# A linear-attention scan feeding an FFN: a different written order for the first 42 FFN tasks and the work around them

## The chip, the cores and the metric

One core of a Trainium2 chip runs the whole program. It has TensorE (PE, with its weight loads shown as PEld), VectorE (DVE), ScalarE (ACT), GpSimd (POOL) and SyncE (SP), which here only issues transfers. The metric is the device time of one execution in microseconds (us). "Runs" below are executions that were timed; the profile is of one execution.

## The reference

For every batch and head a 48x48 state is carried over 768 time steps, and the result goes through an FFN with a sigmoid-approximated GELU.

```
for t in range(S):                                   # r,k,v,w: (4, 8, 768, 48), u: (8, 48)
    cur = einsum('bhd,bhe->bhde', u[None] * kt, vt)
    y[:, :, t] = einsum('bhd,bhde->bhe', rt, state + cur)
    state = wt[:, :, :, None] * state + einsum('bhd,bhe->bhde', kt, vt)
x = y.transpose(0, 2, 1, 3).reshape(3072, 384)
h = x @ w_in                                         # (3072, 384) @ (384, 2048)
g = h * (1 / (1 + exp(-1.702 * h)))
out = g @ w_out                                      # (3072, 2048) @ (2048, 384)
```

## The kernel before, in words

The 3072 tokens are 24 chunks of 128. A chunk `t` is one run of the generator `chunk`, which yields between 13 parts. In order they are: a scan on DVE (L330, with the small L333); a second scan (L335); the product kq (L341); four transposes on PE (L348) and their copy kt on ACT (L350); rku (L356, DVE); ps_d (L368, PE); the copy s and eight small am operations on ACT (L371, L378); ps_u (L398, L402, PE); the state (L408 to L412, DVE); a predicated copy into am (L415, DVE); ps_y (L425, L438, PE) and a one-element copy on ACT that follows it (L448); the other half of L438; and the split of the result into a high and a low part x (L271 on ACT, L272 on DVE). Chunks 0 and 1 are kept whole instead (L462), and split later (L471, L473). From chunk 8 on rku and ps_d are replaced by L359 to L361 and L383 on DVE.

The FFN runs as tasks: task `j` is a group of chunks and one of 16 blocks of the hidden width. Its first product on PE is `g` (L502 to L504: high weights by both halves of x, low weights by the high half), its GELU is `h` (L519 and L520 on ACT, and the difference gl on DVE, L522), its second product is `y` (L540 to L542). Tasks 0 to 4 are done in plain float32 (L497, L512, L537) before their weights are split. Tasks 0 to 9 cover two chunks (256 columns), task 10 and later four chunks (512).

Weights arrive in 12 pieces of 1024 KB: `f` issues the transfer of a piece into one of three staging buffers, `w` converts it in four parts (L253 and L254 on ACT; L256 and L259 on DVE; the high part on ACT, L263; the low part on DVE, L267). The last DVE instruction of the second part lets the buffer go. `l` issues the loads of a chunk, `m` is a check sum on ACT (L277), `x` moves 16 rows of finished x between partitions with small transfers from SP and POOL (L481), `s` splits chunks 0 and 1, `d` followed by a number arranges that the next PSUM bank taken is first written by that many products of a constant tile (L305, "warm", 128x512 in bfloat16, results never used). Five PSUM banks go round, first freed, first taken; a bank is free when ACT or DVE has read it.

Engines run their instructions in the order in which the program issues them. That order is written out by hand in the string `RAMP`: each token is one part of the above (`a3` is the next part of chunk 3, `g5` the first product of task 5). After its last token, which belongs to task 41, a rule (`rest`) gives the order of the remaining tasks. Every queue is in order, SP's too: a load that waits for its buffer holds up the loads behind it.

Of the kernel before, what the change touches and what calls it, by code (L numbers as in the profile page):

```python
# [79 lines left out]
BEFORE = 9  # L80
FIRST = 42
RAMP = """
l0 M l1 l0 a0 a0 a0 d26 a0 l0 a1 a0 d6 a0 f0 m0 a0 a0 l2 a1 l1 a1 l2 a0 a1 m1 a1 d6 a1 l3 a1 a0 a2 a1 a0 a1 a0 a1 w0
l3 a2 a1 a0 a2 a3 d5 a2 a1 a1 f1 w1 f2 x1 a2 a3 d4 a2 a3 a2 a2 l4 a3 a2 a3 d5 a3 w0 f3 a3 a3 a2 a3 m2 a3 g0 h0 g1 w2
l4 w1 a2 h1 a3 w2 a4 a2 f4 w3 a2 w2 w3 a3 a3 x3 y0 y1 w2 g2 g3 h2 w1 h3 f5 g4 w0 h4 a4 s0 y2 w4 w0 y3 y4 m3 g5 s0 a4
w4 h5 w3 w1 a4 w3 a4 w5 g6 h6 g7 g8 g9 l5 w5 h7 y5 f6 w4 l6 f7 w4 a4 a4 a4 h8 a5 w5 y6 f8 w5 y7 h9 a5 w6 g10 g11 g12
h10 y8 y9 a5 y10 h11 w6 w7 h12 w6 a4 w6 y11 a4 a5 a5 g13 h13 g14 f9 y12 w7 m4 g15 l5 a5 w8 h14 a4 w8 h15 w7 a5 w7
g16 g17 y13 a6 h16 y14 y15 y16 w9 a6 h17 w9 f10 f11 g18 g19 m5 h18 a5 w8 a4 a5 h19 a5 w8 w10 y17 a6 l7 w9 y18 y19
w11 g20 a7 l7 w9 a6 a6 w10 h20 g21 g22 w11 h21 w10 l6 w11 a6 a6 y20 w10 w11 a4 h22 u y21 g23 a7 h23 a5 a6 a6 a5 l8
a7 m7 a6 m6 a8 g24 a7 a7 a5 a8 y22 a7 h24 a6 a7 a7 a6 a7 l8 a8 y23 l9 a7 a6 a8 l9 a8 m8 a8 a7 l10 a9 a8 l10 a8 a7 a7  # L90
a9 x7 a9 g25 y24 h25 y25 a9 a9 a8 a8 a10 a10 g26 g27 h26 y26 a9 a9 l11 h27 a8 a9 a9 m9 a8 a10 g28 a11 y27 a9 a10 a10
a10 a10 g29 a8 a11 h28 a9 a10 l11 a9 a11 h29 y28 a10 a11 y29 g30 a11 a9 a11 m10 a10 a11 a11 a11 a11 h30 l12 a10 a11
l13 a10 a10 a11 y30 a12 a12 m11 a11 g31 a12 l14 a13 a13 g32 g33 h31 g34 y31 g35 g36 h32 h33 h34 a13 m12 y32 h35 g37
a12 y33 h36 y34 y35 y36 h37 y37 g38 g39 g40 h38 g41 h39 h40 y38 y39 h41
"""
WIDE = 512
GAP = 64
# [703 lines left out]
```

## Time and profile before

| | |
|---|---|
| runs | 502.23, 501.39, 503.08 us; median 502.23 |
| profiled execution | 501.6 us from the first to the last instruction |
| PE busy | 489.3 us, 98% |
| PE weight loads | 405.8 us, 81% |
| DVE / ACT / POOL busy | 294.2 us (59%) / 227.2 us (45%) / 15.4 us (3%) |
| mean granted TensorE clock | 0.995 of 2.4 GHz |
| moved by DMA | 45.82 MB |

Busy time counts overlapping instructions of an engine once. The page gives the span alone for the profiled execution, and it lies inside the range of the runs. Averages over the whole span hide that the first 160 us and the rest are different: the chunks' and the weights' work on DVE and ACT lies mostly in the first part.

### The profile page before, as it was taken

The numbers are of one execution on the slowest core, as the hardware profiler recorded it, in microseconds if no ns is written. First come the engines' busy times: TensorE is split into PE (matmuls) and PEld (weight loads), VectorE is DVE, ScalarE is ACT, GpSimd is POOL, SyncE is SP. The second block draws the span as 40 slices with busy tenths as digits, with TensorE's granted clock in tenths as the row PEclk, the third lists the DMA queues.
The fourth block names the chain that finished last, engine by engine and source line by source line (L and its number), as shares of the span: only waits on it lengthen the run. The fifth ranks groups of instructions, "written<-read, shape, count | busy, mean of one in ns | idle before, by whom it ended". The sixth has DMA issues, their size and how long they took to land.

```text
span 501.6 us, 11866 instructions
## 1 busy us (share of the span) xinstructions
PE 489.3 (98%) x5036; PEld 405.8 (81%) x5036; DVE 294.2 (59%) x502; ACT 227.2 (45%) x526; POOL 15.4 (3%) x48
## 2 busy tenths in 40 slices
PE   8989999999999999999999999999999999999996
PEld 4668999887887888888888888888888878888884
DVE  8889999989898314765655555655655521111211
ACT  2889899775444324432342442342442332322221
POOL 2001000001001000000001000001000001000000
PEclk9989999999999999999999999999999999999999
DMA  7884988056532500261104171104040001100001
GB/s 200 259 214 138 221 263 226 23 151 185 173 83 55 136 0 3 95 190 48 48 3 126 45 208 49 51 1 126 23 138 1 1 1 31 64 0 0 1 0 70
DMA packets 26508, 45.82 MB, mean 91 GB/s; under 512 B 3952, under 2 KB 17712, under 8 KB 26448
## 3 DMA queue, kind: packets, MB, share of 16 engines
q1 hardware_dynamic: 25472, 42.94, 30.5%
q0 software_dynamic: 864, 1.66, 1.4%
q8 instruction: 41, 0.67, 0.6%
q10 hardware_dynamic: 112, 0.39, 0.3%
q14 instruction: 19, 0.16, 0.1%
HBM read 38.00 MB, written 4.72 MB: 85 GB/s over the span
## 4 chain that ended last, share of the span: by engine, by line
PE 87%; DVE 8%; DMA 2%; issue 1%; ACT 1%; SPq 0%; DVEq 0%; ACTq 0%
PE po L540 12%; PE ph L502 12%; PE ph L504 12%; PE ph L503 12%; PE po L542 12%; PE po L541 12%; PE ps_y L438 2%; PE ps_y L425 2%; PE ps_u L402 2%; PE ph L497 2%; PE ps_u L398 2%; DMA wkr_t<-in_wkr 2%; PE ps_t L348 2%; PE po L537 1%; DVE lp L330 1%
## 5 line engine op out<-in xcount | busy, mean ns | idle before, releaser
L522 DVE TENSOR_TENSOR gl<-gf,gh 128x512 fp32r<-128x512 f32 (+1 forms) x101 | 65.7, 650 | 158.2 <-ACT gf L520 157.2
L519 ACT ACTIVATE gh<-ph 128x512 fp32r<-128x512 f32 (+1 forms) x101 | 57.1, 566 | 204.9 <-PE ph L504 193.8
L502 PE MATMUL ph<-x,h 128*128 128x512 f32 (+1 forms) x303 | 115.6, 382 | 0.7 <-DVE am L415 0.7
L504 PE MATMUL ph<-x,l 128*128 128x512 f32 (+1 forms) x303 | 113.4, 374 | 0.0
L540 PE MATMUL po<-gh,h 128*128 128x512 f32 (+1 forms) x297 | 113.3, 381 | 0.0
L503 PE MATMUL ph<-x,h 128*128 128x512 f32 (+1 forms) x303 | 113.2, 373 | 0.0
L542 PE MATMUL po<-gl,h 128*128 128x512 f32 (+1 forms) x297 | 111.2, 374 | 1.2 <-DVE gl L522 1.2
L541 PE MATMUL po<-gh,l 128*128 128x512 f32 (+1 forms) x297 | 110.9, 374 | 0.0
L502 PEld LDWEIGHTS ph<-x,h 128*128 128x128 f32 x303 | 57.0, 188 | 10.8 <-PE po L542 0.9
L542 PEld LDWEIGHTS po<-gl,h 128*128 128x128 f32 x297 | 55.9, 188 | 12.0 <-DVE gl L522 1.9
L504 PEld LDWEIGHTS ph<-x,l 128*128 128x128 f32 x303 | 57.0, 188 | 10.4
L503 PEld LDWEIGHTS ph<-x,h 128*128 128x128 f32 x303 | 57.1, 188 | 9.6
L540 PEld LDWEIGHTS po<-gh,h 128*128 128x128 f32 x297 | 55.9, 188 | 10.4
L541 PEld LDWEIGHTS po<-gh,l 128*128 128x128 f32 x297 | 56.0, 188 | 9.3
L520 ACT ACTIVATE gf<-ph 128x512 f32<-128x512 f32 (+1 forms) x101 | 56.7, 562 | 4.6 <-DVE gl L522 4.6
L330 DVE TENSOR_TENSOR_SCAN lp<-wkr_t,d1r 112x516 f32<-112x516 f32 x24 | 29.4, 1226 | 1.0 <-DMA wkr_t<-in_wkr 1.0
L341 DVE TENSOR_TENSOR kq<-wkr_t,lp 112x1024 f32<-112x1024 f32 x24 | 29.3, 1221 | 0.9 <-PE ps_y L438 0.6
L335 DVE TENSOR_TENSOR_SCAN lp<-wkr_t,d1f 112x516 f32<-112x516 f32 x24 | 29.5, 1229 | 0.5
L350 ACT COPY kt<-ps_t 128x448 f32<-128x448 f32 (+1 forms) x24 | 12.7, 530 | 34.4 <-PE ps_t L348 34.4
L277 ACT ACTIVATE junk<-lp 112x1032 bf16<-112x1032 f32 x24 | 25.5, 1063 | 0.0
L438 PE MATMUL ps_y<-kq,mid 64*64 64x64 f32 (+3 forms) x384 | 22.9, 218 | 0.8 <-ACT mid L448 0.4
L481 POOL DMA_DIRECT2D x<-x x18 | 9.0, 507 | 380.1 <-DVE x L272 269.2
(101 smaller groups left out, 517.5 us busy)
## 6 DMA issues: line engine op xcount, KB each, us to landing
st<-in_w_out SPq DMA_DIRECT2D x6, 1024.0 KB, 6.0
rk_t<-in_vrk SPq DMA_DIRECT2D x16, 384.0 KB, 4.3
st<-in_w_in SPq DMA_DIRECT2D x6, 896.0 KB, 8.6
v_t<-in_vrk SPq DMA_DIRECT2D x24, 192.0 KB, 3.7
out_t<-ob SPq DMA_DIRECT2D x15, 256.0 KB, 2.3
wkr_t<-in_wkr SPq DMA_DIRECT2D x18, 192.0 KB, 3.2
wkr_t<-in_wkr SPq DMA_DIRECT2D x36, 96.0 KB, 3.4
wkr_t<-in_wkr SPq DMA_DIRECT2D x5, 577.9 KB, 4.8
```

The costliest lines, as they stand in the source:

```text
L330: V.tensor_tensor_scan(li[:, ::-1], w1[:, ::-1], d1r.rearrange("r p c -> r (p c)")[:, ::-1], 0.0, op0=ALU.mult, op1=ALU.add)
L335: V.tensor_tensor_scan(pm, w0, d1f.rearrange("r p c -> r (p c)"), 0.0, op0=ALU.mult, op1=ALU.add)
L438: T.matmul(ps[b][head(h), p], from_[head(half), p * D + OFF * h : p * D + HB], qf[head(half), p, blocks[b]], start=False, stop=p == PAIRS[ ...
L502: T.matmul(ph, h_, xs[i][:, 0, c, cs], start=c == 0, stop=False)
L503: T.matmul(ph, h_, xs[i][:, 1, c, cs], start=False, stop=False)
L504: T.matmul(ph, l_, xs[i][:, 0, c, cs], start=False, stop=c == NM - 1)
L519: A.activation(gh, ph, AF.Gelu_apprx_sigmoid, scale=1.0 / W_SCALE)
L520: A.activation(gf, ph, AF.Gelu_apprx_sigmoid, scale=1.0 / W_SCALE)
L522: V.tensor_tensor(gl, gf, gh.bitcast(F32), op=ALU.subtract)
L540: T.matmul(o, h_, gh, start=first, stop=False, skip_group_check=True)
L541: T.matmul(o, l_, gh, start=False, stop=False, skip_group_check=True)
L542: T.matmul(o, h_, gl, start=False, stop=f == NF - 1, skip_group_check=True)
```

## The change

The string `RAMP` is replaced. Both strings issue the same parts of the same chunks, pieces and tasks, and end at the same point, so the program after task 41 is the same. Only the order differs, and the numbers behind `d`: 52 dummy products before (26, 6, 6, 5, 4, 5), 60 after (36, 1, 9, 3, 1, 3, 2, 2, 3). No function changes.

```diff
 RAMP = """
-l0 M l1 l0 a0 a0 a0 d26 a0 l0 a1 a0 d6 a0 f0 m0 a0 a0 l2 a1 l1 a1 l2 a0 a1 m1 a1 d6 a1 l3 a1 a0 a2 a1 a0 a1 a0 a1 w0
-l3 a2 a1 a0 a2 a3 d5 a2 a1 a1 f1 w1 f2 x1 a2 a3 d4 a2 a3 a2 a2 l4 a3 a2 a3 d5 a3 w0 f3 a3 a3 a2 a3 m2 a3 g0 h0 g1 w2
...
+d2 d34 l0 M l0 a0 a0 l0 l1 a0 a0 a0 d1 f0 l2 l1 m0 a0 a0 a0 a1 a1 a1 a0 a0 d9 a1 a1 a1 m1 a1 a1 a0 a0 a2 a1 a2 l3 l2 w0
+a1 d3 a0 a1 a2 a3 a0 a1 a1 f1 a2 a2 a3 w1 l3 f2 x1 d1 a3 a2 a2 a2 a3 l4 a3 w0 a3 d3 f3 a3 l4 m2 a2 a2 a3 a3 a3 g0 h0
...
```

SP issues the transfers. In these rows, from some 12 us to some 26 us, `wkr_t` and `v_t` are a chunk's inputs, `st` a weight piece and the last row of shuffles the `x` of chunks 0 and 1. Before:

```order
L214 DMA v_t_86<-in_vrk 128x384
L198 DMA wkr_t_83<-in_wkr 96x1541
L214 DMA v_t_84<-in_vrk 128x384
L235 DMA st<-in_w_out 128x2x1024
L233 DMA st<-in_w_in 112x2x1024
L233 DMA st<-in_w_in 16x2x1024
L481 DMA l_384<-l_384 16x256 x3
```

After:

```order
L198 DMA wkr_t_83<-in_wkr 96x1541
L214 DMA v_t_86<-in_vrk 128x384
L235 DMA st<-in_w_out 128x2x1024
L214 DMA v_t_84<-in_vrk 128x384
L233 DMA st<-in_w_in 112x2x1024
L233 DMA st<-in_w_in 16x2x1024
L481 DMA l_399<-l_399 16x256 x3
```

The piece of w_out has moved ahead of the load into `v_t_84`, which has to wait until ps_y of chunk 0 has read that buffer. Further down the same queue the piece `f5` has moved ahead of the shuffles of chunks 2 and 3 (`x3`) in the same way.

DVE, around 33 to 43 us, behind the am copies of chunk 3; `h_416` and `h_425` are piece 1, `l_580` and `l_582` piece 2. Before:

```order
L256 SCALAR_TENSOR_TENSOR st<-st 128x1024
L259 SCALAR_TENSOR_TENSOR h_416<-h_416,st 128x1024
L256 SCALAR_TENSOR_TENSOR st<-st 128x1024
L259 SCALAR_TENSOR_TENSOR l_580<-l_580,st 128x1024
L330 SCALAR_TENSOR_TENSOR lp<-wkr_t_82,d1r 112x516
L333 RECIPROCAL d1f<-lp 112x4
L272 TENSOR_TENSOR x<-ps_y_586,x 112x4x64
```

After:

```order
L256 SCALAR_TENSOR_TENSOR st<-st 128x1024
L259 SCALAR_TENSOR_TENSOR h_425<-h_425,st 128x1024
L330 SCALAR_TENSOR_TENSOR lp<-wkr_t_82,d1r 112x516
L333 RECIPROCAL d1f<-lp 112x4
L256 SCALAR_TENSOR_TENSOR st<-st 128x1024
L259 SCALAR_TENSOR_TENSOR l_582<-l_582,st 128x1024
L272 TENSOR_TENSOR x<-ps_y_617,x 112x4x64
```

The first scan of chunk 4 now stands between the two pieces. Just behind, the product kq of chunk 4 (L341) has moved ahead of the low part of piece 0 (L267), and the split of chunks 0 and 1 (L473) behind it.

PE, ahead of ps_y of chunk 4 (some 75 us). Before:

```order
L502 MATMUL ph<-x,h_847 128x256
L503 MATMUL ph<-x,h_847 128x256
L504 MATMUL ph<-x,l_859 128x256
L368 MATMUL ps_d<-hm,rku 128x2 x4
L425 MATMUL ps_y_1131<-am,v_t_85 48x64
```

After:

```order
L540 MATMUL po_650<-gh,h_949 128x256
L541 MATMUL po_650<-gh,l_951 128x256
L542 MATMUL po_650<-gl,h_949 128x256
L305 LDWEIGHTS warm
L305 MATMUL ps_y_1126<-warm 128x512
L305 LDWEIGHTS warm
L305 MATMUL ps_y_1126<-warm 128x512
L425 MATMUL ps_y_1126<-am,v_t_85 48x64
```

Two dummy products stand there now, and the second product of task 12 comes before ps_y instead of after it. In the same way two dummies stand before the transposes of chunk 8 and three before ps_y of chunk 7.

## Rows read from the trace of the kernel before

**Rows 1.** The page: busy time of the engines.
```profile
PE 489.3 (98%) x5036; PEld 405.8 (81%) x5036; DVE 294.2 (59%) x502; ACT 227.2 (45%) x526; POOL 15.4 (3%) x48
```

**Rows 2.** Windows: length, then busy us of PE, PEld, DVE, ACT, POOL, clock, DMA.
```profile
200.00:250.00 50.00, 50.00 (x565) 41.32 (x564) 31.50 (x65) 19.41 (x44) 0.00 (x0) 1.00 0.33 96
```

**Rows 3.** Waits from 0 to 165 us: us in total, times, longest.
```profile
ACT st L253 <- DMA st<-in_w_out: 2.3, 3, 1.0
PE po L542 <- DVE gl L522: 1.2, 2, 0.9
```

**Rows 4.** Timeline of PE at the start: begin, length, instruction, idle before.
```profile
1.14 7.46 PE L305 MATMUL ps_t<-warm 128*128 128x512 bf16 x26 [1.14 <-DVE warm L119]
9.39 0.57 PE L348 MATMUL ps_t<-ident,kq 112*128 112x112 f32 x4 [0.79 <-DVE kq L341]
12.22 0.62 PE L398 MATMUL ps_u<-v_t,kt 64*64 64x48 f32 x30
```

**Rows 5.** Timeline of PE's weight loads, from the first rise of the clock.
```profile
4.53 3.57 PEld L305 LDWEIGHTS <-warm 128*128 128x128 bf16 x17 [0.28 <-issue]
```

**Rows 6.** Timeline of DVE, 14 to 21 us.
```profile
14.84 0.36 DVE L412 TENSOR_TENSOR sf<-ps_u,mid 112x192 f32<-112x192 f32 x1 [1.25 <-ACT mid L406]
20.89 1.23 DVE L341 TENSOR_TENSOR kq<-wkr_t,lp 112x1024 f32<-112x1024 f32 x1
```

**Rows 7.** Timeline of ACT, 10 to 15 us.
```profile
10.43 1.07 ACT L277 ACTIVATE junk<-lp 112x1032 bf16<-112x1032 f32 x1
12.59 2.02 ACT L378 ACTIVATE am<-same,s 128x64 f32<-128x64 f32 x8
```

**Rows 8.** Issues on SP, timeline.
```profile
18.91 0.43 SPq L235 DMA_DIRECT2D st<-in_w_out  x1
24.30 1.88 SPq L481 DMA_DIRECT2D l<-l  x3
```

**Rows 9.** DMA issues up to 165 us: times, size of one, median us to landing.
```profile
x<-x POOLq DMA_DIRECT2D x3, 32.0 KB, 2.0
l<-l POOLq DMA_DIRECT2D x3, 16.0 KB, 6.3
```

**Rows 10.** Windows: the last three columns are clock, share of DMA engines, GB/s.
```profile
16.00:20.00 4.00, 3.64 (x138) 3.47 (x142) 3.76 (x10) 3.32 (x13) 0.00 (x0) 1.00 0.69 177
20.00:31.00 11.00, 9.70 (x222) 7.03 (x216) 10.52 (x15) 9.20 (x31) 1.60 (x3) 1.00 0.99 261
41.00:46.00 5.00, 5.00 (x25) 4.40 (x24) 4.96 (x8) 4.74 (x12) 0.89 (x2) 1.00 0.00 0
```

**Rows 11.** Timeline of PE, 27 to 46 us.
```profile
27.08 1.24 PE L305 MATMUL ps_d<-warm 128*128 128x512 bf16 x5
30.13 0.62 PE L398 MATMUL ps_u<-v_t,kt 64*64 64x48 f32 x30 [0.71 <-ACT s L371]
31.62 4.51 PE L497 MATMUL ph<-l,l 128*128 128x256 f32 x12 [0.33 <-DVE am L415]
41.70 4.05 PE L497 MATMUL ph<-l,l 128*128 128x256 f32 x18
```

**Rows 12.** Windows of one microsecond.
```profile
32.00:33.00 1.00, 1.00 (x4) 0.82 (x3) 0.90 (x4) 1.00 (x2) 0.00 (x0) 0.50 0.45 162
```

**Rows 13.** Timeline of DVE, 36 to 51 us.
```profile
36.89 1.23 DVE L256 SCALAR_TENSOR_TENSOR st<-st 128x1024 int32<-128x1024 int32 x1 [1.27 <-ACT l L254]
48.13 0.95 DVE L473 TENSOR_TENSOR x<-l,x 128x768 fp32r<-128x768 f32 x1
50.13 1.22 DVE L256 SCALAR_TENSOR_TENSOR st<-st 128x1024 int32<-128x1024 int32 x1
```

**Rows 14.** Timeline of PE: task 5 begins, and two waits later on.
```profile
49.28 0.47 PE L502 MATMUL ph<-x,h 128*128 128x256 f32 x1
72.67 0.36 PE L502 MATMUL ph<-x,h 128*128 128x256 f32 x1 [0.68 <-DVE am L415]
82.09 0.39 PE L542 MATMUL po<-gl,h 128*128 128x256 f32 x1 [0.32 <-DVE gl L522]
```

More of the change, by code (lines that the diff above doesn't have):

```diff
@@ L82 @@
 RAMP = """
-l0 M l1 l0 a0 a0 a0 d26 a0 l0 a1 a0 d6 a0 f0 m0 a0 a0 l2 a1 l1 a1 l2 a0 a1 m1 a1 d6 a1 l3 a1 a0 a2 a1 a0 a1 a0 a1 w0
-l3 a2 a1 a0 a2 a3 d5 a2 a1 a1 f1 w1 f2 x1 a2 a3 d4 a2 a3 a2 a2 l4 a3 a2 a3 d5 a3 w0 f3 a3 a3 a2 a3 m2 a3 g0 h0 g1 w2
-l4 w1 a2 h1 a3 w2 a4 a2 f4 w3 a2 w2 w3 a3 a3 x3 y0 y1 w2 g2 g3 h2 w1 h3 f5 g4 w0 h4 a4 s0 y2 w4 w0 y3 y4 m3 g5 s0 a4
-w4 h5 w3 w1 a4 w3 a4 w5 g6 h6 g7 g8 g9 l5 w5 h7 y5 f6 w4 l6 f7 w4 a4 a4 a4 h8 a5 w5 y6 f8 w5 y7 h9 a5 w6 g10 g11 g12
-h10 y8 y9 a5 y10 h11 w6 w7 h12 w6 a4 w6 y11 a4 a5 a5 g13 h13 g14 f9 y12 w7 m4 g15 l5 a5 w8 h14 a4 w8 h15 w7 a5 w7
@@ L88 @@
[L88 to L92, printed above, removed]
@@ L93 @@
-l13 a10 a10 a11 y30 a12 a12 m11 a11 g31 a12 l14 a13 a13 g32 g33 h31 g34 y31 g35 g36 h32 h33 h34 a13 m12 y32 h35 g37
-a12 y33 h36 y34 y35 y36 h37 y37 g38 g39 g40 h38 g41 h39 h40 y38 y39 h41
+d2 d34 l0 M l0 a0 a0 l0 l1 a0 a0 a0 d1 f0 l2 l1 m0 a0 a0 a1 a1 a1 a0 a0 d9 a1 a1 a1 m1 a1 a1 a0 a0 a2 a1 a2 l3 l2 w0
+a1 d3 a0 a1 a2 a3 a0 a1 a1 f1 a2 a2 a3 w1 l3 f2 x1 d1 a3 a2 a2 a2 a3 l4 a3 w0 a3 d3 f3 a3 l4 m2 a2 a2 a3 a3 a3 g0 h0
+g1 w2 w1 a2 a4 a3 h1 w2 y0 a2 a3 f4 g2 w3 a3 w3 f5 w1 w2 a2 w0 g3 x3 y1 a4 g4 h2 h3 h4 l5 w2 y2 w4 s0 y3 a4 f6 w0 w3
@@ new lines @@
+y4 w4 s0 g5 h5 w1 m3 a4 g6 h6 a4 w5 g7 l6 g8 y5 a4 w3 f7 w5 w4 h7 w4 a4 g9 h8 a5 a4 y6 y7 g10 w5 w5 h9 a5 w6 y8 g11 y9
+h10 a5 y10 h11 w6 g12 g13 w7 a4 h12 g14 w6 a5 w6 f8 h13 w8 y11 a4 g15 a5 m4 w7 d2 h14 y12 w8 a4 w7 a5 h15 g16 w7 f9 l5
+a5 a6 y13 y14 h16 f11 w9 a6 g17 h17 y15 a4 g18 w9 y16 f10 m5 g19 h18 a5 l7 w8 a5 a5 y17 h19 y18 w9 w10 w8 y19 a6 w11
+g20 a6 w9 g21 w10 h20 w11 g22 l6 a6 w10 h21 w11 a7 l7 h22 y20 w11 a6 a6 y21 a5 w10 g23 a4 a7 h23 a6 u a5 a7 a6 m6 l8
+m7 a6 a8 g24 a7 a7 a5 a8 y22 a7 h24 a6 a7 a7 a6 a7 l8 y23 a8 d2 a6 a8 l9 a7 l9 a8 m8 d3 a7 l10 a8 a9 a8 a8 a7 a7 g25
@@ L95 @@
+x7 a8 y24 a9 h25 a9 y25 a8 a9 a9 g26 h26 g27 y26 l10 a9 a10 a9 a10 h27 a8 a9 a9 a8 m9 y27 a10 a8 l11 a11 g28 a9 a10
+a11 a10 h28 a10 g29 a9 a10 a10 l11 a9 y28 a11 h29 a10 a11 y29 g30 a11 a9 m10 a10 a11 a11 a11 a11 a11 h30 l12 a10 a11
+a12 y30 a12 l13 a10 a12 l14 a11 a11 m11 g31 a10 g32 h31 a13 g33 g34 g35 m12 a13 g36 y31 h32 h33 a13 h34 y32 h35 a12
+y33 h36 y34 g37 g38 y35 y36 h37 y37 g39 g40 h38 h39 h40 g41 y38 h41 y39
 """
```

## The prediction

> **What bounds the kernel.** The page first: PE is busy for 98% of the span, the others far less [rows 1]. Busy PE is not PE at its best, so I looked at windows: in a stretch well behind the change PE is busy for all of 50 us at the full clock [rows 2]. What the change can move therefore lies in the first 160 us, as dummy products, waits and slow clock on PE. Everything PE needs there less than before ends the kernel earlier by as much, since the later tasks follow each other without a gap.
>
> The list of waits and PE's timeline say where this is. At the start PE runs 26 dummies and then waits for the first kq [rows 4]. Around 30 us it waits for ps_u of chunk 3 and for the first real task [rows 11], and that task runs at half clock: 0.50 granted, 1.2 of 2.4 GHz [rows 12]. Its 12 products took 4.51 us, where later 18 took 4.05 [rows 11], so some 1.8 us are lost. Later there are three waits for DVE: 0.68 us at 72.67, 0.32 at 82.09 [rows 14] and one of 0.9, the longest for gl [rows 3]; its place in the timeline is near 124 us. Between 20 and 100 us DVE hardly rests, and its own largest idle stretch after the start is 1.27 us at 36.89, waiting for ACT [rows 13]. That is the limit which I followed through the new order.
>
> **The start.** The dummies begin at 1.14. From 4.53 on their weights follow each other at 3.57/17 = 0.21 us [rows 5], so ten more hold the first transposes from 9.39 [rows 4] to about 10.6. PE gets most of this back: five dummies fewer follow, and rku now comes right behind the first kq, so that ps_u of chunk 0 starts near its old 12.22 [rows 4]. ACT doesn't: the check sum of 1.07 us starts 1.04 us behind the transposes [rows 4, 7], now at 11.65, ends at 12.75 or so with its small read, and only then come s and the eight am of 2.02 us, so that am starts at about 12.95 in place of 12.59 [rows 7]. DVE, which waits for ACT there, gets going again at 15.2, not 14.84 [rows 6]. Moving the second scan of chunk 2 ahead of an am copy hides a short latency between scan and kq, so I take **+0.2 us** at the kq that stood at 20.89 [rows 6]; the bounds are 0.1 and 0.4.
>
> **Transfers to the first task.** The piece of w_out was issued at 18.91 [rows 8] behind a load that waits for ps_y of chunk 0. Now it stands behind a load without a wait and goes out near 17. From 16 to 20 us the DMA engines were 0.69 busy, from 20 to 31 us 0.99 [rows 10]: 0.31 x 4 = 1.2 us of room, so all that follows lands up to 1.2 us earlier. Two things gain. ACT waited up to 1.0 us for such a piece [rows 3], which put off kt and s of chunk 3, hence ps_u at 30.13 [rows 11]; I put it at 29.6. And the shuffles of chunks 0 and 1, issued from 24.30 on [rows 8], took 6.3 us where the same shuffles later took 2.0 [rows 9]; they landed between about 31 and 32 us, which is when the first task began (the row names a DVE copy that ended at the same moment). Both together let the task start at about 30.7 instead of 31.62: **-0.9 us on PE**, between 0 and -1.2.
>
> **The clock.** Before its fall PE had run five dummies from 27.08, then small products with a wait of 0.71 [rows 11]. Now three dummies stand right before ps_u of chunk 3 and the real products follow sooner, so I expect this slow stretch not to come back, worth up to 1.8 us on PE. The Trainium skill (TensorE: Matmul & The Clock Gate, Seeing it yourself and the parts before it) says that the number of slow matmuls at a kernel's start differs from run to run; one profile cannot show it here. By that rule the place of a fall is not the order's alone; it is a rival below.
>
> **DVE to task 5.** The 1.27 us of idle time [rows 13] is ACT's conversion of piece 2. Now the scan of chunk 4 (1.2 us) stands there, ACT is ahead, and the wait goes. What DVE had done before 50.13, without L473 of 0.86 net (48.13 to the next row at 48.99), must be done before task 5 has its low weights: 50.13 - 0.86 - 1.27 - 0.2 (a short wait at the x splits) + 0.2 (start) = 48.0 [rows 13]. PE would arrive at 47.8 without the slow clock: from 30.7, ten plain products of six rows at 4.05/18 = 0.225 [rows 11] are 13.5 us, chunks 2 and 3 take some 2.7 and a wait for piece 2 about 0.8. Task 5 began at 49.28 [rows 14]: **-1.3 us**. With the slow clock PE comes at 48.6: -0.7.
>
> **The later places.** Task 15's bank used to be the one that the am copy of chunk 4 frees, hence the wait at 72.67; by the order of takes and releases it now gets the bank of a kt copy on ACT: **-0.7 us**. The wait at 82.09 I take as gone with DVE's lead: **-0.3 us**. The two dummies at ps_y of chunk 4 cost 2 x 0.21 = **+0.4 us**, the two and three at chunks 8 and 7 **+1.1 us**, against the wait of 0.9 near 124 us which PE, later by as much, no longer has: **-0.9 us**. Dummies are free where PE would wait anyway, and cost their full time where it would not; at the first pair I see no wait, at the second group I see one of nearly their size.
>
> **The sum:** -1.3 - 0.7 - 0.3 + 0.4 + 1.1 - 0.9 = -1.7. On the profiled 501.6 that is 499.9. The median of the runs lies 0.6 above that execution, so I predict **500.5 us**. A measurement of this kernel tells about 0.3%, 1.5 us, from no change, so 500.7 is the limit for faster and 503.7 for slower; the forecast stands almost on the first.
>
> **The rivals.**
> *Clock elsewhere.* The slow stretch falls on the first tasks as before, or just ahead of them where the new order has fewer dummies (one for chunk 2 and none ahead of ps_d of chunk 3, where four and five stood). Task 5 then comes at 48.6: -1.1 in all, 501.1.
> *Shuffles behind f5.* Piece `f5` now goes out ahead of the shuffles of chunks 2 and 3, in a stretch in which the DMA engines rested, 0.00 from 41 to 46 us [rows 10]. Had they the 6.3 us of the first shuffles instead of 2.0 [rows 9], task 5 would begin near 51, 1.7 later than before; with -0.4 from the later places that is 502.2 + 1.7 - 0.4 = 503.5. One piece in flight, where there were two, speaks for less: half of the 4.3 us more would still be hidden. The Trainium skill (DMA: Bandwidth & Descriptors, Issuing engines are not separate DMA queues) says that the transfers of all issuing engines share 16 DMA engines, so issuing some of the shuffles from POOL would be no way past f5; POOL's 6.3 us [rows 9] agree.
> *PE pays for the dummies.* On the other side: ps_y of chunk 4, L348 of chunk 8 and ps_y of chunk 7 come when PE has work, 7 x 0.21 = 1.5 us, the start costs 0.4 and task 5 is no earlier: 502.2 + 1.9 = 504.1. It decides once task 5 starts at 49.3 or later while the waits for gl and am stay.
> *All waits go.* The dummies lie in waits and cost nothing: -1.3 - 0.7 - 0.3 - 0.9 = -3.2, 499.0.
>
> **The numbers.** Forecast 0.40 (its own range 499.8 to 501.2), clock 0.18, f5 0.15, dummies 0.14, all waits 0.13. Faster by over 0.3%: 0.26 of the forecast, all of the last case and 0.04 of the clock's, 0.43. Slower: the dummies' 0.14 and 0.02 of f5's, 0.16. Within: 0.41. The range runs from 498.8 to 503.6 and leaves out the dummies' case and the end of the last one.
>
> **What would show it.** Right: first transposes near 10.6; L497 from about 30.7 in rows of 0.225 us with the clock at 1.00; no DVE idle over 0.5 between 34 and 40 us; task 5 near 48.0; no wait at the L502 that stood at 72.67; no gap before L542 near 122. Wrong: a granted 0.50 anywhere from 14 to 36 us; task 5 after 49.3; dummies late in the ramp with no idle before or behind them while L542 still waits for gl.

## The result: 0.5% slower

| | before | after |
|---|---|---|
| median of 19 runs each | 502.76 us (501.39 to 507.62) | 505.99 us (503.01 to 508.60) |
| ratio, 95% interval | | 1.0051 (1.0029 to 1.0072) |
| profiled execution | span 501.6 us, mean clock 0.995 | span 503.5 us, mean clock 0.993 |

The quotient of the two medians alone is 1.0064, inside the interval. I had forecast 500.5 (498.8 to 503.6), with 0.16 on slower. The execution profiled after took 505.4 us, so 1.9 us of the time lie outside the span. Its clock is better than that of the other runs of after, whose median is 0.990, so this profile is one of the kinder ones.

The page after, which answers to [rows 1], tells no more than its counterpart.

```profile
PE 492.0 (98%) x5044; PEld 406.6 (81%) x5044; DVE 293.8 (58%) x502; ACT 226.9 (45%) x526; POOL 15.4 (3%) x48
```

PE's timeline after has the loss. Up to ps_u of chunk 0 it does what I said: transposes at 10.52 (10.6 forecast), ps_u at 12.00. Then the first task comes at 33.62, where 30.7 was forecast and 31.62 stood before [rows 11], and task 5 at 50.70, where 48.0 was forecast and 49.28 stood [rows 14].

```profile
1.14 9.54 PE L305 MATMUL ps_t<-warm 128*128 128x512 bf16 x36 [1.14 <-DVE warm L119]
10.52 0.55 PE L348 MATMUL ps_t<-ident,kq 112*128 112x112 f32 x4
...
12.00 0.62 PE L398 MATMUL ps_u<-v_t,kt 64*64 64x48 f32 x30
...
29.25 1.44 PE L305 MATMUL ps_u<-warm 128*128 128x512 bf16 x3 [0.56 <-ACT s L371]
31.71 1.00 PE L398 MATMUL ps_u<-v_t,kt 64*64 64x48 f32 x30 [1.03 <-ACT s L371]
...
33.62 3.58 PE L497 MATMUL ph<-l,l 128*128 128x256 f32 x12
...
50.70 0.47 PE L502 MATMUL ph<-x,h 128*128 128x256 f32 x1
```

PE waits twice for s, an ACT copy: 0.56 us for s of chunk 2 (29.04 in the rows below), which frees the bank of the three dummies, and 1.03 us for s of chunk 3 (31.56). ACT's timeline says what holds up both: the w_out piece f1, for 2.04 us, where the longest such wait before was 1.0 [rows 3]. No wait stands before the first task itself, which follows ps_u of chunk 3 at once.

```profile
26.83 1.21 ACT L253 ACTIVATE st<-st 128x1024 int32<-128x1024 uint32 x1 [2.04 <-DMA st<-in_w_out]
27.91 1.14 ACT L254 ACTIVATE h<-st 128x1024 f32<-128x1024 f32 x1
28.95 0.19 ACT L254 ACTIVATION_READ_ACCUMULATOR h<-st 128x1 f32 x1
29.04 0.15 ACT L371 COPY s<-ps_d 128x8 f32<-128x8 f32 x1
...
31.56 0.16 ACT L371 COPY s<-ps_d 128x8 f32<-128x8 f32 x1
```

SP's issues after: f1 goes out at 16.92, as early as I had said (18.91 before [rows 8]). But v of chunk 2, the row at 16.44, now stands behind the wkr load of chunk 3, which waits for its buffer until 16.07. The first two rows of SP's order in the section on the change show this move; the text there names only the one of the w_out piece.

```profile
9.93 0.32 SPq L198 DMA_DIRECT2D wkr_t<-in_wkr  x1
10.30 0.43 SPq L214 DMA_DIRECT2D v_t<-in_vrk  x1
16.07 0.32 SPq L198 DMA_DIRECT2D wkr_t<-in_wkr  x1
16.44 0.44 SPq L214 DMA_DIRECT2D v_t<-in_vrk  x1
16.92 0.43 SPq L235 DMA_DIRECT2D st<-in_w_out  x1
19.08 0.34 SPq L214 DMA_DIRECT2D v_t<-in_vrk  x1
```

Windows after (columns as in [rows 2] and [rows 10]): from 15 to 17 us the DMA engines are busy for 0.30 of the time, then for all of it up to 31 us. And the clock is at 0.50, 1.2 of 2.4 GHz, from 28.3 to 35.1 us, twice as long as before (3.4 us, from 31.9 to 35.3), so my forecast of no slow stretch was wrong.

```profile
15.00:17.00 2.00, 1.40 (x13) 1.18 (x11) 1.73 (x5) 1.43 (x3) 0.00 (x0) 1.00 0.30 67
17.00:20.00 3.00, 2.57 (x112) 2.36 (x113) 2.76 (x6) 2.93 (x13) 0.00 (x0) 1.00 1.00 260
20.00:31.00 11.00, 9.00 (x165) 6.13 (x163) 10.62 (x16) 8.07 (x25) 1.60 (x3) 0.88 1.04 254
28.30:35.10 6.80, 5.21 (x74) 3.58 (x74) 4.68 (x12) 6.45 (x23) 0.00 (x0) 0.50 1.01 220
```

The same two microseconds before, where v of chunk 2 had been issued ahead of that wait:

```profile
15.00:17.00 2.00, 1.69 (x23) 1.18 (x23) 2.00 (x5) 1.35 (x4) 0.00 (x0) 1.00 0.84 197
```

DVE after, against [rows 6, 13]: the start costs it 0.25 to 0.34 us (sf at 15.09, kq at 21.23), within my bounds. The 1.27 us of idle time at piece 2 is gone, as forecast, but a wait of 1.78 for ps_u of chunk 3 and one of 0.93 at the x splits have come instead.

```profile
15.09 0.36 DVE L412 TENSOR_TENSOR sf<-ps_u,mid 112x192 f32<-112x192 f32 x1 [1.30 <-ACT mid L406]
...
21.23 1.22 DVE L341 TENSOR_TENSOR kq<-wkr_t,lp 112x1024 f32<-112x1024 f32 x1
...
33.75 0.36 DVE L409 TENSOR_TENSOR mid<-ps_u,sf 112x192 f32<-112x192 f32 x1 [1.78 <-PE ps_u L402]
...
38.92 1.23 DVE L256 SCALAR_TENSOR_TENSOR st<-st 128x1024 int32<-128x1024 int32 x1
...
42.34 0.79 DVE L272 TENSOR_TENSOR x<-ps_y,x 112x256 fp32r<-112x256 f32 x2 [0.93 <-ACT x L271]
```

The waits at 72.67 and 82.09 [rows 14] are gone. Late in the ramp the five dummies of chunks 8 and 7 come at 117.30 and 118.13, and there is no wait for gl behind them, but one of 0.71 us without a releaser (the last section comes back to it).

```profile
117.30 0.60 PE L305 MATMUL ps_t<-warm 128*128 128x512 bf16 x2
...
118.13 0.81 PE L305 MATMUL ps_y<-warm 128*128 128x512 bf16 x3
...
123.26 0.50 PE L502 MATMUL ph<-x,h 128*128 128x512 f32 x1 [0.71 <-issue]
```

### The profile page after: what moved, and what is told of

It is laid out like the page before. It is cut to its first block, busy times and chain, and to the rows that moved or that the text cites. A ratio compares the mean times of both kernels' runs of the same rounds, so it can differ in the third digit from the quotient of the medians.

```text
span 503.5 us, 11880 instructions
## 1 busy us (share of the span) xinstructions
PE 492.0 (98%) x5044; PEld 406.6 (81%) x5044; DVE 293.8 (58%) x502; ACT 226.9 (45%) x526; POOL 15.4 (3%) x48
## 4 chain that ended last, share of the span: by engine, by line
PE 94%; DMA 2%; ACT 2%; issue 1%; DVE 1%; SPq 0%; ACTq 0%
PE po L540 13%; PE ph L502 13%; PE ph L504 13%; PE ph L503 13%; PE po L542 12%; PE po L541 12%; PE ps_y L425 3%; PE ps_y L438 2%; PE ps_u L402 2%; PE ps_u L398 2%; PE ps_t L305 2%; DMA st<-in_w_out 2%; PE ps_t L348 2%; PE ph L497 2%; PE po L537 1%; PE po L564 1%
## 5 line engine op out<-in xcount | busy, mean ns | idle before, releaser
L341 DVE TENSOR_TENSOR kq<-wkr_t,lp 112x1024 f32<-112x1024 f32 x24 | 29.3, 1220 | 0.6 <-PE ps_y L438 0.4
L438 PE MATMUL ps_y<-kq,mid 48*48 48x64 f32 (+3 forms) x384 | 23.0, 218 | 0.8 <-ACT mid L448 0.5
```

What stands on the lines that cost most here:

```text
L438: T.matmul(ps[b][head(h), p], from_[head(half), p * D + OFF * h : p * D + HB], qf[head(half), p, blocks[b]], start=False, stop=p == PAIRS[ ...
```

## The experiments

All edits are in the string `RAMP`, and no kernel leaves work out. "After, both" has 26 dummies at the start and v of chunk 2 early; "both" in the rows below it is the same kernel. Each row is of 12 runs ("after, more dummies" of 6). Ratios are to runs of the kernel before that were taken beside these, with 95% intervals, and compare better from row to row than the medians do. 0.1% is 0.5 us.

| kernel | median us | ratio | interval |
|---|---|---|---|
| old start, new order from g1 | 501.69 | 0.9969 | 0.9936 to 1.0003 |
| new start, old order from g1 | 505.11 | 1.0043 | 1.0012 to 1.0075 |
| after, f1 back | 504.62 | 1.0019 | 0.9992 to 1.0047 |
| after, more dummies | 508.41 | 1.0103 | 1.0061 to 1.0145 |
| after, f1 back, more dummies | 506.56 | 1.0058 | 1.0033 to 1.0083 |
| old start with f1 first, new order | 502.98 | 0.9992 | 0.9961 to 1.0023 |
| old start, new order without late dummies | 501.02 | 0.9958 | 0.9931 to 0.9984 |
| after, 26 dummies at the start | 502.90 | 1.0005 | 0.9984 to 1.0026 |
| after, v of chunk 2 early | 503.25 | 1.0010 | 0.9982 to 1.0037 |
| after, both | 501.05 | 0.9969 | 0.9953 to 0.9986 |
| old start with 36 dummies, new order | 504.62 | 1.0042 | 1.0018 to 1.0066 |
| both, without late dummies | 502.09 | 0.9989 | 0.9959 to 1.0019 |
| both, more dummies | 500.96 | 0.9967 | 0.9941 to 0.9993 |
| both, 20 dummies at the start | 503.35 | 0.9998 | 0.9972 to 1.0025 |

**Which half.** Up to `g1` the two orders issue the same parts but for one load, so they can be joined there. (In the diff of the section on the change, the new first line has one `a0` too many behind `m0`; the kernel has two there.) First the old start with the new order behind it:

```diff
-d2 d34 l0 M l0 a0 a0 l0 l1
+l0 M l1 l0 a0 a0 a0 d26 a0
...
-g1 w2 w1 a2 a4 a3 h1 w2
+g1 w2 l4 w1 a2 a4 a3 h1 w2
```

> The order of before up to the second FFN product g1, the changed order from there on (the seven late dummies among it). Theory 'start': the loss is made before the first FFN tasks (first task at 33.62 us instead of 31.62), so this kernel is within 0.3% of before, at about +0.4 us (the start gains back 1.4 us of the profile's 1.8), and its first L497 stands at 31.6 with task 5 at or before 49.3. Rival 'late dummies': the seven dummies (1.5 us) and the new order behind task 5 are the loss, so it is 1.5 to 3 us slower than before, as the changed kernel is.

and the mirror of it:

> The mirror: the changed order up to g1, the order of before from there on. Theory 'start': slower than before by 1.5 to 3 us (0.3 to 0.6%), first L497 near 33.6, clock at 0.50 from about 28 to 35 us. Rival 'late dummies': within 0.3% of before, whatever the first task does, since the later waits take up what the start loses.

Measured 501.69 and 505.11: the loss is in the start, and the order behind `g1` with its late dummies is no slower. PE and DVE of the old start with the new order:

```profile
31.71 2.86 PE L497 MATMUL ph<-l,l 128*128 128x256 f32 x12
...
48.05 0.47 PE L502 MATMUL ph<-x,h 128*128 128x256 f32 x1
```

```profile
37.02 1.23 DVE L256 SCALAR_TENSOR_TENSOR st<-st 128x1024 int32<-128x1024 int32 x1
```

No idle time stands before piece 2, and task 5 begins at 48.05, the 48.0 of my DVE step, from a first task that starts where it did before.

**f1's place.** f1 goes back behind v of chunk 3:

```diff
-a1 a1 f1 a2 a2 a3 w1 l3 f2
+a1 a1 a2 a2 a3 l3 f1 w1 f2
```

> The changed kernel with one thing undone: the w_out piece f1 stands behind the load of v of chunk 3 again, as in before. Theory 'f1 out of place': ACT's 2.04 us of waiting for f1 shrinks to about 1, the first L497 stands near 32, and the time is 1.5 to 2 us below the changed kernel. Rival 'DMA engines': f1 was issued 2 us earlier in the changed kernel and still had 11 of 16 engines done at 23.5 us, the last five only by 26.8; if those stragglers are not made by f1's place, the first task stays at 33 or later and the time does not move by more than 0.5 us.

Measured 504.62; in its profile f1 lands at 27.1, though 15 of 16 DMA engines are done by 25.5, ACT still waits 1.77 us and the first task starts at 33.94. The runs are lower by 0.32 points of a per cent, with intervals that overlap, and the mechanism I named is not there. The unedited kernel again, one execution:

> The changed kernel once more, unedited, for a second profile. Theory 'order': f1 lands within 0.5 us of 26.80 again, its last five engines 2 to 3 us behind the others, the clock falls near 28.3, the first L497 is within 0.3 us of 33.62. Rival 'differs from execution to execution': the stragglers, the landing of f1 and the place and length of the 0.50 stretch differ by over a microsecond from the first profile.

It took 507.56. f1's last engines lagged again (26.5 us). The clock didn't repeat: it first rose at 5.45 us instead of 4.41, and was at 0.50 for 13.7 us from 25.9 on instead of 6.8. Nor did DVE's step: a wait of 1.09 us for ACT stands before piece 2 (39.74 us), and task 5 begins at 53.21. The mirror puts f1 first in the old start:

```diff
-a1 w0 l3 a2 a1 a0 a2 a3 d5 a2 a1 a1 f1 w1
+a1 w0 f1 l3 a2 a1 a0 a2 a3 d5 a2 a1 a1 w1
```

> The mirror of the transfer theory: the old start with only f1 moved ahead of the load of v of chunk 3, as in the changed kernel, and the new order behind g1. It was my step that f1 then lands up to 1.2 us earlier. Theory 'f1's place decides': some engines lag by 2 to 3 us again, f1 lands at 26 or later though it is issued near 16.2, ACT waits 1.5 us or more, and the time is 1 to 2 us above the 501.7 of the kernel with the old start. Rival 'v of chunk 2 and the other moves': f1 lands before 24.5, ACT waits less than 0.5 us, the first task starts at 31 or earlier and the time is the same or lower.

Here f1 landed at 24.97 (25.7 without the edit), ACT waited 0.56 instead of 1.38, and the first task came 0.5 us earlier, at 31.17, as I had argued in the prediction. That is no more than two executions of one start differ by: in the kernel without late dummies below, which has the same old start and f1 in its old place, f1 landed at 24.92 and the first task came at 30.91. The time, 502.98, is not distinguishable from 501.69. f1's place alone is not the cause.

**Dummies ahead of chunks 2 and 3.**

```diff
-x1 d1 a3 a2 a2 a2 a3 l4 a3 w0 a3 d3 f3 a3
+x1 d4 a3 a2 a2 a2 a3 l4 a3 w0 d5 a3 f3 a3
```

> The changed kernel with the dummies around chunks 2 and 3 as they were before: four in place of one ahead of ps_d of chunk 2, five ahead of ps_d of chunk 3 in place of three ahead of its ps_u. f1 stays ahead of v of chunk 3. Theory 'too few dummies': the stretch at 0.50 that three profiles of this early order show from about 26 to 28.4 us, 6.8 to 13.7 us long, goes or is 3.5 us at most, and the time falls by 1.5 to 2.5 us against the changed kernel. Theory 'late transfers': ACT still waits 1.5 to 2 us for f1, PE has then nothing to do at 29 to 31 whatever the dummies are, the clock falls all the same and the time is within 0.7 us of the changed kernel's.

> Both together: f1 behind the load of v of chunk 3, and the dummies as before. If transfers and dummies are the whole loss of the start, this is within 0.3% of the kernel with the old start and the new order behind it (501.7 us), with a first L497 near 31.7 and no stretch at 0.50 over 3.5 us. If the ten more dummies at the start, the later load of v of chunk 2 or the other moves cost something, 1 us or more is left.

Both got slower, 508.41 and 506.56, though their profiles show only 3.4 us at 0.50: too few dummies was not the cause either. Part of what the extra dummies cost is a wait without a releaser near 124 us, 1.55 and 1.87 us long, where the kernels without them have 0.71 and 0.42 (last section):

```profile
124.70 0.50 PE L503 MATMUL ph<-x,h 128*128 128x512 f32 x1 [1.55 <-issue]
```

The profile of the first pointed at the start. DVE's sf, with its wait for ACT:

```profile
16.39 0.36 DVE L412 TENSOR_TENSOR sf<-ps_u,mid 112x192 f32<-112x192 f32 x1 [2.46 <-ACT mid L406]
```

It comes 1.3 us later than after, because the clock first rose at 7.04 us there and the 36 dummies ended at 12.0, not 10.7.

**The start's dummies and the late load.** Three edits of the changed kernel:

```diff
-d2 d34 l0 M l0 a0 a0
+d2 d24 l0 M l0 a0 a0
```

> The changed kernel with 26 dummies at the very start, as before, in place of 36; nothing else. In the profiles so far the first rise of the clock lies anywhere from 4.4 to 7.0 us; before it a dummy takes 0.43 us, behind it 0.21. So 36 of them end at 10.5 us when the clock rises at 4.4 and at 11.8 when it rises at 7.0, 26 of them at 8.4 and 9.6, and the first kq is there at 9.4. Theory 'the 36 delay the whole start, more so in most executions than in the profile I read': first transposes at 9.4 to 9.6, first task 1 us or more earlier, the median 1 to 2 us below the changed kernel's 506. Rival 'PE gets it back, as I predicted' (+0.2 us): no more than 0.5 us below.

```diff
-f0 l2 l1 m0 ... a2 l3 l2 w0
+f0 l2 l1 l2 m0 ... a2 l3 w0
```

> The changed kernel with one load moved back: v of chunk 2 ahead of the wkr load of chunk 3, which waits for its buffer until about 16 us. In the changed kernel the DMA engines were idle then (busy share 0.42 and 0.09 in 15 to 17 us) and all from v of chunk 2 on came at once behind it. Theory 'idle DMA': f1 lands 0.7 to 1.5 us earlier (25.5 or before), ACT's wait for it shrinks to 1 us or less, the time falls by 0.7 to 1.5 us. Rival: the stragglers of f1 stay, f1 lands at 26 or later, no change over 0.4 us.

> Both edits, 26 dummies and v of chunk 2 early, f1 ahead as in the changed kernel. If the start's loss is these two, this is within 1 us of the kernel with the old start and f1 first (503.0, profile 500.0 span), first L497 near 31.2; if the stretches at 0.50 are a loss of their own (one and three dummies in place of four and five ahead of chunks 2 and 3), one of 3 to 7 us is still there and the time is 1 to 2 us above it.

Measured 502.90, 503.25 and, with both, 501.05: against after 0.46, 0.41 and 0.82 points of a per cent, 2.3, 2.1 and 4.1 us, so the two add up. From the intervals of the table each of these differences is uncertain by some 0.3 points, 1.5 us: the dummies and the two together are clear of noise, the load alone only just. With v of chunk 2 early and still 36 dummies the weight loads and PE read:

```profile
6.56 3.77 PEld L305 LDWEIGHTS <-warm 128*128 128x128 bf16 x18 [0.17 <-issue]
```

```profile
11.53 0.55 PE L348 MATMUL ps_t<-ident,kq 112*128 112x112 f32 x4
...
32.17 3.62 PE L497 MATMUL ph<-l,l 128*128 128x256 f32 x12
```

The clock rose at 6.45, the transposes stand a whole microsecond behind those after, and yet the first task starts 1.45 us earlier: f1 landed 6.5 us after its issue at 17.47, where after it took 9.9. With both edits PE, SP and the windows read:

```profile
9.66 0.55 PE L348 MATMUL ps_t<-ident,kq 112*128 112x112 f32 x4
...
30.77 2.92 PE L497 MATMUL ph<-l,l 128*128 128x256 f32 x12
...
47.18 0.47 PE L502 MATMUL ph<-x,h 128*128 128x256 f32 x1
```

```profile
10.42 0.91 SPq L214 DMA_DIRECT2D v_t<-in_vrk  x2
15.22 0.34 SPq L198 DMA_DIRECT2D wkr_t<-in_wkr  x1
15.60 1.55 SPq L235 DMA_DIRECT2D st<-in_w_out  x1
```

```profile
15.00:17.00 2.00, 1.66 (x56) 1.68 (x59) 1.91 (x4) 1.93 (x6) 0.00 (x0) 1.00 0.81 204
```

The first task begins at 30.77, my 30.7, although the clock rose only at 7.04: with 26 dummies the transposes then stand 0.3 us behind their old 9.39 [rows 4], no more. The mirror, 36 dummies in the old start:

```diff
-l0 M l1 l0 a0 a0 a0 d26 a0
+l0 M l1 l0 a0 a0 a0 d36 a0
```

> The mirror: the old start with 36 dummies in place of 26, the new order behind g1. Theory 'the 36 delay the start': transposes at 10.5 to 11.8 in place of 9.4, task 5 1 to 2 us behind the 48.05 of the same kernel with 26, time 1 to 2 us above its 501.7. Rival 'PE gets it back': within 0.5 us of 501.7.

Measured 504.62, 0.73 points (3.7 us, uncertain by some 2) above the same kernel with 26, and DVE waits 3.03 us for ACT at sf:

```profile
16.55 0.36 DVE L412 TENSOR_TENSOR sf<-ps_u,mid 112x192 f32<-112x192 f32 x1 [3.03 <-ACT mid L406]
```

**The late dummies.** First in the kernel with the old start, then in the one with both edits:

```diff
-m4 w7 d2 h14 ... y23 a8 d2 a6 ... m8 d3 a7
+m4 w7 h14 ... y23 a8 a6 ... m8 a7
```

> The old start with the new order behind it, without the seven late dummies (2 ahead of the bank of ps_y of chunk 4, 2 and 3 at chunks 8 and 7). Theory 'PE pays for them': 1.0 to 1.5 us below the 501.7 of the same kernel with them. Rival 'they lie in waits': within 0.5 us of it, with waits of that size for gl, am or kq where the dummies stood.

> The changed kernel with 26 dummies at the start, v of chunk 2 early, and without the seven late dummies (ps_y of chunk 4, chunks 8 and 7). My term for them was +0.4 and +1.1 us, less 0.9 for a wait near 124 us. Theory 'they are covered': in the trace the start of the last tasks moves by 0.2 us or less against the same kernel with them, the time by less than 0.5 us. Rival 'PE pays': 1.0 to 1.5 us below 501.05.

501.02 beside 501.69, 502.09 beside 501.05: the runs show no saving like the 1.5 us that the dummies take. In the second pair of traces task 5 comes 1.54 us later without the late dummies (PE waited 1.44 us for s ahead of the first task); behind the place of the first two it is 1.08 later, behind that of the other five still 1.09. So the two cost 0.46 us and the five nothing: where they stood, PE now waits for kt,

```profile
116.07 0.66 PE L425 MATMUL ps_y<-am,v_t 64*48 64x64 f32 x30 [0.65 <-ACT kt L350]
```

and 0.11 for gl behind it. The first pair gives 0.46 for the two and nothing for the five as well; what it loses again, 0.55 us at 96.5, is lost 20 us ahead of the five, where PE waits 0.30 us for rku.

**The rest of the clock.** The edit of "more dummies" again, now on the kernel with both edits, and a kernel with 20 dummies in place of 26 at the start (`d2 d18`):

> The changed kernel with 26 dummies at the start, v of chunk 2 early, and four and five dummies ahead of ps_d of chunks 2 and 3 in place of one there and three ahead of ps_u of chunk 3. Theory 'the half-clock stretch comes from too few dummies': it goes (mean clock 0.998 or more), the first real task runs at full clock and the time is 0.5 to 1 us below 501.05. Rival 'the dummies delay the chain': ps_d of chunks 2 and 3 come later by up to 0.6 us each, the time is 0.5 us or more above 501.05, as it was above the changed kernel when I made the same edit there (508.4 against 506.0).

> The changed kernel with v of chunk 2 early and 20 dummies at the start. Theory 'only dummies that end behind kq cost': 26 end at 9.66 us when the clock rises at 7.0, 0.3 us behind kq, and earlier else; 20 end at 8.4 at the latest, so nothing is left to win: within 0.4 us of 501.05, and PE waits about 1 us for kq. Rival 'fewer are worse': with PE idle ahead of the transposes the clock falls or rises later, transposes and small products run at half clock to 10 us and beyond, 0.5 to 2 us above 501.05.

With more dummies 500.96: no slow stretch is left in the profile (mean clock 1.000, span 498.5 instead of 498.9), the first task starts at 29.93, and the time is the same within its interval.

```profile
29.93 2.83 PE L497 MATMUL ph<-l,l 128*128 128x256 f32 x12 [0.44 <-DVE sf L412]
```

```profile
17.00:36.00 19.00, 17.51 (x412) 14.32 (x404) 18.13 (x31) 17.48 (x53) 1.61 (x3) 1.00 0.87 250
```

With 20 dummies 503.35, 0.29 points above 26, with intervals that overlap. In the profile PE waits 2.78 us for kq, and then runs the transposes' successors at half clock:

```profile
9.71 0.57 PE L348 MATMUL ps_t<-ident,kq 112*128 112x112 f32 x4 [2.78 <-DVE kq L341]
```

```profile
10.60:17.40 6.80, 6.80 (x80) 4.31 (x80) 6.39 (x11) 3.60 (x13) 0.00 (x0) 0.50 0.81 197
```

So of the three numbers tried at the start 26 is the best: 36 delay kq's users, and with 20 the clock fell, though the runs don't set 20 and 26 apart for certain.

## Why the prediction was wrong

**The start (+0.2 forecast): failed.** It took one profile's first rise of the clock, the 4.53 of [rows 5], for a property of the kernel. In the 17 profiles of this case the rise lies between 3.81 and 7.04 us, in 13 of them behind 5.4. A dummy takes 0.43 us before it, 0.22 behind it. With 26 dummies most of a late rise lies inside the wait of 0.79 for kq [rows 4]; with 36 there is no such wait left, and each microsecond of a later rise shifts transposes, ACT and DVE by half of one (transposes at 10.52 with the rise at 4.41, at 11.82 with the rise at 7.04). In the profile after, with a rise at 4.41, the step looks right; the runs pay 2.3 us (0.46 points) for the ten dummies in the new start, and 3.7 in the old one. Part of that comes 110 us later, as the wait without a releaser at 123.26 us, which no kernel with 26 or 20 dummies in the new start has. The Trainium skill (TensorE: Matmul & The Clock Gate, What's actually happening) warns not to fit a model to one count of slow products, since it differs between runs of one kernel; the rises at 4.41 and 5.45 in the two profiles of the changed kernel agree. I had cited that page for the later stretch and not for this step, which needed it.

**Transfers (-0.9 at the first task): failed.** f1 was issued when I said, but it found work ahead of it that I had not counted: v of chunk 2 had moved behind the wkr load of chunk 3, and the step's list of loads that changed places with a waiting one was not complete. The "1.2 us of room" between 16 and 20 us was nearly used up by the idle stretch that this opened from 15 to 17 us, (0.84 - 0.30) x 2 = 1.1 us. That is not all: eleven of the 16 DMA engines had finished their parts of f1 by 23.50, where before fifteen had by 24.12, and the other five, up to 26.80, held up ACT and with it s and the first task. Undoing the one move gives 2.1 us, and with the start undone too the first task stands at 30.77. How the move makes single engines lag isn't shown (last section).

**The clock (up to 1.8 gained): wrong.** The slow stretch came back, 6.8 us long. The dummies ahead of chunks 2 and 3 were not its whole cause, since adding them to the changed kernel only made it slower. With transfers and start in order they remove it, for a gain that the runs can't tell from none. How much of the loss is slow clock can be estimated from the mean clocks of 303 runs of 16 kernels (they leave out the time before the first rise). A straight line of time against mean clock, with one slope for all and a level for each kernel, gives 3.8 us for a hundredth of the clock, which is 10 us at 0.50. After has 0.991 on average and before 0.996, so 2.0 us of the loss go with the clock. At equal clock the ten dummies cost 3.1 us in the new start and 3.0 in the old one, and the changed order with 26 of them is 2.4 us faster than before, for a forecast of 1.7. The early load gains 1.0 us beside 36 dummies and 0.1 beside 26, so most of its gain goes with the clock. Each of these estimates is uncertain by 0.5 to 0.7 us.

**DVE to task 5 (-1.3): right in mechanism, where the start is on time.** In the kernels with the new order behind `g1` and the first task at 31.71 or earlier the idle time went, and task 5 stood at 46.65 to 48.72, for 49.28 before. With a late start other waits on DVE came, 2.7 us of them after, and the idle time at piece 2 itself came back in two profiles: 1.09 us in the second of the changed kernel and 1.64 with more dummies there.

**The later places (-0.7, -0.3, +0.4, +1.1, -0.9): single terms close, their sum not shown.** Waits at 72.67 and 82.09 gone; two dummies 0.46 for 0.4; the five at 117 us and the wait for gl come to no loss, for a loss of 0.2. From task 5 to a product late in the program (488.28 us before) the new order gains 0.63 us behind the old start, for my 0.4; but the old order behind the new start gains 0.58 on the same stretch, so single traces can't give this to the new order. Behind the new start the new order loses 0.35, of which the wait of 0.71 without a releaser is the visible part.

**The sum.** Its 0.6 between the profiled execution and the median compares run times with a span, and a span lies 1.7 to 1.9 us below the time of its execution; what it amounts to is 502.23 - 1.7, the same 500.5.

**The rivals.** None was what happened as a whole. "Clock elsewhere" named what came, a slow stretch just ahead of the first tasks, from 28.3 us on, but priced it with task 5 at 48.6, and it began at 50.70. "PE pays for the dummies" has the right side and nearly the right time (504.1), but names the wrong dummies: the late ones are covered, those at the start aren't. "Shuffles behind f5" is out: the shuffles of chunk 3 landed some 2.2 us after their issue. What stays open is why the time of after spreads over 5.6 us: the granted clock goes with it (0.998 at 503.01, 0.984 at 508.60), but what decides it in an execution isn't seen.

## What to carry to other kernels

Dummy products that keep a clock up must be counted at the slow rate, against the wait they fill, and over several executions: a number that just fits in one profile delays everything in the others. Look at what they do far behind their place, too: here the ten cost a wait 110 us later. When a load moves in a queue, look for the idle stretch that opens behind the load that waits, not only at the load that goes out earlier. And a kernel that is put together from both orders (here the changed one with 26 dummies and v of chunk 2 early, 0.9969 of before) can be better than either.

## What the hardware showed that I had not expected

In four profiles in which v of chunk 2 and f1 went out in a row behind the idle stretch (after, its repetition, the new start with the old order, and the one with more dummies), the 16 DMA engines finished their parts of f1 far apart: after, eleven by 23.5 us and the last at 26.80. With 26 dummies and v late two lagged, up to 24.4; with v early and 36 dummies none, all were done between 23.5 and 24.0. But v's place doesn't decide it alone: with v early and 20 dummies five lagged again, up to 24.63 where eleven were done by 22.24, and with both edits and no late dummies two, up to 24.79. The records don't say what held them up.

The clock fell to 0.50 at 28.30 us after although PE's longest wait since 20 us had been 0.33 us, and at 10.63 in the kernel with 20 dummies after a wait of 2.78 us.

PE's waits without a releaser have a pattern. Behind the first 10 us the 17 profiles hold 13 of them over 0.1 us, up to 1.87 us long. Each ends 1.35 to 1.54 us after a 16 KB packet that the profile lists as an instruction transfer has landed (after, the packet landed at 121.74 and PE went on at 123.26), and they stand only before PE's products number 221, 349, 476 and 1618, counted from the start with the dummies, whatever work these are. That reads as PE waiting for its next instructions. The eight waits at product 1618 are all in profiles with 59 dummies or more (nine profiles); the eight profiles with 55 or fewer have none there. No edit was made to try this, but it is a price of dummy products that my sum did not have.
